# First two pieces' q, k, v loaded into the last weights' space, weights prepared wide and in place, and a new order of the opening

## The chip, the core and the metric

The kernel runs on one core of a Trainium2 chip (trn2). The metric is the device time of one execution in microseconds. Matmuls run on TensorE (PE, with its weight loads as PEld), element-wise work on VectorE (DVE), ScalarE (ACT) and GpSimd (POOL); all loads and stores are issued from SyncE's queue (SP).

## What is computed

Three stages follow each other: windowed attention, a gated MLP behind an RMS norm, and a second MLP with a softmax-like gate and a layer norm. The weights come as 64-bit floats, since a 32-bit array is scaled by a NumPy 64-bit scalar.

```python
# attention: B, H, S, D = 4, 8, 576, 64
scores = scale * np.matmul(q, k.transpose(0, 1, 3, 2))
mask_plain = (rel >= 0) & (rel < 32)                       # heads 0 to 3
mask_dil = (rel >= 0) & (rel < 128) & (rel % 4 == 0)       # heads 4 to 7
attn = softmax(np.where(masks, scores, -1e9)); out = attn @ v
# first MLP: 2304 tokens, 512 -> 1536 -> 512
xn = x / np.sqrt(np.mean(x * x) + 1e-6) * rms_g
y = (silu(xn @ w_gate) * (xn @ w_val)) @ w_out
# second MLP: 512 -> 1024 -> 512
h = y @ w_in;  solu = h * softmax(h)
out = ((solu - mean) / sqrt(var + 1e-6) * g_ln) @ w_out
```

## The kernel before

The 2304 tokens are cut into nine **pieces** of 256 (line 26). The attention of a piece is done in groups of eight heads' query blocks; a group is one load of q and k, one load of v, and a chain: `scores` (TensorE, into PSUM `sp`), `maximum`, `centred`, `exps`, `sums`, `norm`, `weights`, `transposes` (TensorE, `tp`), two scaled copies `turned0` and `turned1` (`pT`), `values` (TensorE, `pv`), `copy` into `x`. The pieces 0 and 1 have four groups each, with a mask added by a matmul (`first`); they are the opening. `rms` then squares `x`, sums over the model's width with matmuls (`ms`), takes the root on GpSimd, spreads it over the partitions with a matmul (`rs`), scales `x`, and splits it into a high and a low part (`xh`, `xl`) in fp32r, so that a product in full precision is three matmuls (`mm3`, lines 603 to 606).

The first MLP works on 12 blocks f of 128 hidden units. For each f there are `g` and `vp` (the two input products, one PSUM bank each), then tanh on ScalarE, two products and the high-low split on VectorE and ScalarE (`u`, `uh`), and `y` (the output product). The table `VIRTUAL` says which tokens and f go together: piece 0 with f=0 to 2 at 256 columns, piece 1 with f=0 to 2, then both together with f=3 to 11 at 512 columns, then the later pieces. The attention of the later pieces is spread between these matmuls.

The weights are in 64 bits and are turned on the chip, in 36 blocks of 512 (f times gate, value, output), by `prepare`: a fetch of 512 KB (`raw_w`), `shifted` on ScalarE (high words, into `tf`), `parts` on VectorE (low words shifted right, into `wf`; line 276), `joined` on VectorE (line 280), `halves` on ScalarE (the high part, `h_w`), and `lows` on VectorE or GpSimd (the difference; line 250, the helper `less`). `tf` and `wf` have two and four buffers. The second MLP's 16 blocks go the same way, each after the last use of the block whose space it takes.

The order on every engine is set by a **planner**, `Plan`: each step has a list of steps that it needs, buffers that it takes, a cost on each engine that may do it and a due time; the planner runs these through a list schedule and writes the instructions in the order that comes out. Each engine works its instructions strictly in that order. While the planner expects TensorE to be idle, ahead of the first `spread`, the main loop writes filler matmuls (`warm`, line 858) into its stream. q, k and v have two buffers each, so the third group's load waits for the first group's scores.

Of the kernel before, what the change touches and what calls it, by code (L numbers as in the profile page):

```python
# [105 lines left out]
class Plan:  # L106
# [3 lines left out]
    SLACK = {"t": 0.3, "s": 0.2}  # L110
# [12 lines left out]
    def order(self):  # L123
# [73 lines left out]
def tile_attention_glu_solu(ctx: ExitStack, tc: tile.TileContext, qk_d, v_d, w1_d, win2_d, wout2_d,  # L197
# [20 lines left out]
    seed = const.tile([P, 1], BF16, name="seed")  # L218
    rmsg = const.tile([P, KD], F32, name="rmsg")
# [9 lines left out]
                 "sq": 2, "rs": 1, "u": 2, "uh": 2, "yo": 2, "wf": 4, "bh": 1, "bl": 1, "ch": 1, "cl": 1,  # L229
                 "yl": 3, "yh": 3} | {f"w{f}_{i}": 1 for f in range(NF1) for i in range(3)})  # L230
# [25 lines left out]
    def prepare(key, tag, src, scale, due, needs=()):
        k, raw, tf, wf, th = ((x, key) for x in ("k", "raw", "tf", "wf", "th"))

        def fetch(e):
            r = T[raw] = wp.tile([P, 512, 2], I32, tag=tag, name=f"raw_{tag}")  # L260
            nc.sync.dma_start(out=r.rearrange("p n t -> p (n t)"), in_=src.bitcast(I32))

        def shifted(e):


            nc.scalar.activation(new(stg, tf, [P, 512], name="tf"), T[raw][:, :, 1].bitcast(F32), AF.Prelu,
                                 scale=2.0 ** -112, alpha=-2.0 ** 32)

        def wf_():
            return T["wf", key[0]][:, plan.where[wf][1]]  # L270

        def parts(e):

            if ("wf", key[0]) not in T:
                T["wf", key[0]] = xn.tile([P, 4, 512], F32, tag="cl0", name="wf")
            nc.vector.tensor_scalar(wf_().bitcast(U32), T[raw][:, :, 0].bitcast(U32), 29, None, ALU.logical_shift_right)

        def joined(e):
            w = wf_().bitcast(U32)
            nc.vector.scalar_tensor_tensor(out=w, in0=T[tf].bitcast(U32), scalar=3, in1=w,  # L280
                                           op0=ALU.logical_shift_left, op1=ALU.bitwise_or)

        def scaled(e):
            put(e, wf_(), wf_(), scale)

        def halves(e):

            T[th] = wp.tile([P, 2, 512], F32R, tag=tag, name=f"h_{tag}")
            put(e, T[th][:, 0], wf_())

        def lows(e):
            less(e, T[th][:, 1], wf_(), T[th][:, 0])
            (w1 if key[0] == 1 else w2)[key[1:]] = T[th]

        plan.add((key, "fetch"), {"s": 1.6}, fetch, needs, due=due - 12)
        plan.add((key, "shifted"), {"a": 0.68}, shifted, [(key, "fetch")], takes=[("yo", tf)], due=due)
        lead = (key[0],) + ((0, 0) if key[0] == 1 else (0,))
# [663 lines left out]
```

## Time and profile before

| | |
|---|---|
| median of 3 runs | 780.44 us (779.95 to 780.68) |
| the profiled execution | 782.46 us, span 780.7 us |
| TensorE busy | 98% of the span |
| VectorE, ScalarE, GpSimd busy | 53%, 40%, 14% |
| mean granted TensorE clock | 0.987 |
| read from HBM | 58.71 MB |

The profile is one execution, seen by the hardware profiler. Its span is from the first to the last instruction; the profiled execution's own time is a little longer and stands beside the runs' times. The busy share of TensorE says little here, since matmuls are pipelined and fillers count as work; more is to be read from when a certain matmul starts. The granted clock is the share of full clock that TensorE got in a stretch.

### The profile page before, as it was taken

To read this page: it belongs to the slowest core of one execution; us is meant where nothing else is said; L and a number is where in the kernel's file an instruction comes from. 1 tells how busy PE (TensorE), PEld (TensorE's weight loads), DVE (VectorE), ACT (ScalarE), POOL (GpSimd) and SP (SyncE) were. 2 spreads that over 40 slices of the span, in tenths; PEclk is the share of its full clock that TensorE was granted. 3 is DMA by queue.
4 is the path that set the end of the run, shared out by engine and by line. 5 is a ranking of instruction groups with operands and counts; after the bars stand their busy time and mean duration, and the time that the engine had idled before them with its cause. 6 is when DMAs were issued, how large, how long until landed. Compare 5 with 4: busy or idle time off the path is not lost.

```text
span 780.7 us, 12092 instructions
## 1 busy us (share of the span) xinstructions
PE 763.8 (98%) x4775; PEld 634.7 (81%) x4775; DVE 416.3 (53%) x838; ACT 315.8 (40%) x781; POOL 111.2 (14%) x150
## 2 busy tenths in 40 slices
PE   8799999999999999999999999999999999999997
PEld 6689887789997778887788888888878888888886
DVE  4769999754444344434353438962254445444542
ACT  3456676444333333324333325531144433434432
POOL 0121033321120121211110200200011101101100
PEclk9869999999999999999999999999999999999999
DMA  8999022242014201033211027500101101111101
GB/s 260 318 384 372 22 73 72 76 130 73 14 33 134 71 27 49 1 100 124 73 41 50 1 83 241 176 28 0 68 1 54 55 28 54 54 29 55 40 28 41
DMA packets 34234, 68.94 MB, mean 88 GB/s; under 512 B 3329, under 2 KB 13569, under 8 KB 34177
## 3 DMA queue, kind: packets, MB, share of 16 engines
q1 hardware_dynamic: 34176, 68.16, 26.1%
q8 instruction: 38, 0.62, 0.3%
q14 instruction: 20, 0.16, 0.1%
HBM read 58.71 MB, written 9.44 MB: 87 GB/s over the span
## 4 chain that ended last, share of the span: by engine, by line
PE 89%; DVE 5%; DMA 2%; issue 1%; ACT 1%; POOL 1%; SPq 0%; ACTq 0%; POOLq 0%; DVEq 0%
PE vp L604 7%; PE y L604 6%; PE vp L606 6%; PE vp L605 6%; PE g L604 6%; PE y L605 6%; PE g L606 6%; PE y L606 6%; PE g L605 6%; PE h L745 4%; PE h L743 4%; PE h L744 4%; PE o L784 4%; PE o L783 4%; PE o L782 4%; PE pv L416 3%
## 5 line engine op out<-in xcount | busy, mean ns | idle before, releaser
L604 PE MATMUL y<-uh,h_w 128*128 128x512 f32 (+1 forms) x252 | 94.0, 373 | 1.0 <-ACT uh L241 1.0
L605 PE MATMUL y<-uh,h_w 128*128 128x512 f32 (+1 forms) x252 | 91.4, 363 | 0.1
L606 PE MATMUL y<-uh,h_w 128*128 128x512 f32 (+1 forms) x252 | 91.2, 362 | 0.0
L640 DVE SCALAR_TENSOR_TENSOR u<-u,g 128x512 f32<-128x512 f32 (+1 forms) x63 | 38.4, 610 | 94.1 <-ACT u L634 93.7
L604 PE MATMUL vp<-xh,h_w 128*128 128x512 f32 (+1 forms) x204 | 81.7, 400 | 0.0
L604 PE MATMUL g<-xh,h_w 128*128 128x512 f32 (+1 forms) x204 | 79.5, 390 | 0.0
L606 PE MATMUL g<-xh,h_w 128*128 128x512 f32 (+1 forms) x204 | 77.7, 381 | 0.3 <-POOL h_w L250 0.3
L605 PE MATMUL g<-xl,h_w 128*128 128x512 f32 (+1 forms) x204 | 77.7, 381 | 0.2 <-DVE xl L250 0.2
L606 PE MATMUL vp<-xh,h_w 128*128 128x512 f32 (+1 forms) x204 | 77.7, 381 | 0.0
L605 PE MATMUL vp<-xl,h_w 128*128 128x512 f32 (+1 forms) x204 | 77.6, 380 | 0.0
L634 ACT ACTIVATE u<-g 128x512 f32<-128x512 f32 (+1 forms) x63 | 33.9, 538 | 85.6 <-PE g L606 85.2
L241 ACT CAST uh<-u 128x512 fp32r<-128x512 f32 (+1 forms) x63 | 35.3, 560 | 74.0 <-DVE u L644 73.9
L644 DVE SCALAR_TENSOR_TENSOR u<-u,vp 128x512 f32<-128x512 f32 (+1 forms) x63 | 38.4, 609 | 47.6 <-PE vp L606 47.4
L381 ACT ACTIVATE s<-s,nm 128x64 f32<-128x64 f32 x120 | 40.6, 341 | 47.9 <-DVE nm L367 47.9
L743 PE MATMUL h<-h_w,yh 128*128 128x512 f32 x144 | 58.2, 404 | 0.0
L784 PE MATMUL o<-h_w,lt 128*128 128x512 f32 (+1 forms) x152 | 57.9, 381 | 0.2 <-DVE lt L772 0.2
L782 PE MATMUL o<-h_w,lt 128*128 128x512 f32 (+1 forms) x152 | 57.7, 380 | 0.0
L783 PE MATMUL o<-h_w,lt 128*128 128x512 f32 (+1 forms) x152 | 57.6, 379 | 0.0
L745 PE MATMUL h<-h_w,yh 128*128 128x512 f32 x144 | 57.0, 396 | 0.0
L744 PE MATMUL h<-h_w,yh 128*128 128x512 f32 x144 | 56.8, 395 | 0.0
L604 PEld LDWEIGHTS y<-uh,h_w 128*128 128x128 f32 x252 | 48.0, 191 | 9.1 <-ACT uh L241 1.2
L500 POOL TENSOR_TENSOR sq<-x 128x256 f32<-128x256 f32 x30 | 19.4, 650 | 249.9 <-DVE x L245 211.0
(115 smaller groups left out, 1552.6 us busy)
## 6 DMA issues: line engine op xcount, KB each, us to landing
raw_w<-w SPq DMA_DIRECT2D x36, 512.0 KB, 10.1
vt<-v SPq DMA_DIRECT2D x38, 256.0 KB, 3.0
qk<-qk SPq DMA_DIRECT2D x20, 400.0 KB, 4.0
y<-yT SPq DMA_DIRECT2D x18, 256.0 KB, 3.0
yT<-yo SPq DMA_DIRECT2D x16, 256.0 KB, 2.3
raw_w<-win SPq DMA_DIRECT2D x8, 512.0 KB, 4.7
raw_w<-wout SPq DMA_DIRECT2D x8, 512.0 KB, 4.3
out<-ob SPq DMA_DIRECT2D x16, 256.0 KB, 2.1
```

Of the source, the lines that this page charges most:

```text
L381: nc.scalar.activation(T[s_][:, i], (T[sp] if first else T[s_])[:, i], AF.Exp, scale=0.125 if first else 1.0, bias=st["nm"][:, i:i + 1], a ...
L604: nc.tensor.matmul(acc, wh, xh, start=first, stop=False)
L605: nc.tensor.matmul(acc, wh, xl, start=False, stop=False)
L606: nc.tensor.matmul(acc, wl, xh, start=False, stop=last)
L640: return lambda e: nc.vector.scalar_tensor_tensor(out=u_of(f), in0=u_of(f), scalar=1.0, in1=T["g", v, f], op0=ALU.add, op1=ALU.mult)
L644: return lambda e: nc.vector.scalar_tensor_tensor(out=u_of(f), in0=u_of(f), scalar=0.5, in1=T["vp", v, f], op0=ALU.mult, op1=ALU.mult)
L743: nc.tensor.matmul(h[:, n], yh[:, 0, k], w[:, 0], start=(k == 0), stop=False)
L744: nc.tensor.matmul(h[:, n], yh[:, 0, k], w[:, 1], start=False, stop=False)
L745: nc.tensor.matmul(h[:, n], yh[:, 1, k], w[:, 0], start=False, stop=(k == KD - 1))
L782: nc.tensor.matmul(o, lt[:, 0, k], w[:, 0], start=(k == 0), stop=False)
L783: nc.tensor.matmul(o, lt[:, 0, k], w[:, 1], start=False, stop=False)
L784: nc.tensor.matmul(o, lt[:, 1, k], w[:, 0], start=False, stop=(k == NF2 - 1))
```

## The change

1. **Loads.** The q, k and v of the first eight groups no longer use the two buffers of the pool but lie in the space of the weights w8 to w11 (`EARLY`), four blocks of the plan's `early_tile`. The loads of w8 to w11 wait for the scores and values that read there; the load of w7 waits for the first piece's split, since that piece's `x` lies in w7's space.
2. **Weights in place.** `shifted` and `parts` write their result over the raw words; `tf` is gone. From f=7 on (`SINGLE`) the three blocks of an f are one tile and each step works on 1536 elements at once. `wf` has two buffers of four blocks. The second MLP's fetches wait for `out` of the f whose space they take.
3. **First piece in PSUM.** Its four `values` results stay in two PSUM banks (`stays`); squares and scalings read them there, and there is no `copy`. All its groups use the `split` form (centre, then one exponential, then a sum). `high` and `low` of `x` work on two of the four blocks at once, for all pieces.
4. **Fillers.** `fill` puts fillers into the bank of the operation that follows, up to 75 us of the plan's time, and adds zeros where the bank is accumulating.
5. **Order.** New costs, due times and slack in the planner; a step's lag to a follower now counts only between engines.

```diff
+EARLY = {(t, n): (NF1 - 1 - 2 * t - n // 2, n % 2) for t in range(2) for n in range(4)}
+X_AT = 7
+SINGLE = 7
+SLACK = {"t": 0.25, "a": 0.4, "d": 0.05, "p": 0.25, "s": 0.2}
+DUE_GROUP, DUE_NEXT, DUE_NORM, DUE_WEIGHTS, DUE_SLOT, DUE_THIRD = (0, 10), 2.23, (7.8, 22.2), 1.47, 4.73, 31.97
+FILL = 75.0
...
+    def fill(x, add=False):
+
+        while filling[0] > 0:
+            filling[0] -= 1
+            nc.tensor.matmul(x, (nothing if add else seed)[:, 0:1].to_broadcast([P, P]),
+                             seed.to_broadcast([P, x.shape[1]]), start=not add, stop=not add)
...
+        def word(c, x):
+            return raw(c)[:, :, :, x]
+
+        def shifted(c):
+
+
+            return lambda e: nc.scalar.activation(word(c, 1).bitcast(F32), word(c, 1).bitcast(F32), AF.Prelu,
+                                                  scale=2.0 ** -112, alpha=-2.0 ** 32)
+
+        def parts(c):
+
+            return lambda e: nc.vector.tensor_scalar(word(c, 0).bitcast(U32), word(c, 0).bitcast(U32), 29, None,
+                                                     ALU.logical_shift_right)
+
+        def joined(c):
+            return lambda e: nc.vector.scalar_tensor_tensor(
+                out=wf_(c).bitcast(U32), in0=word(c, 1).bitcast(U32), scalar=3, in1=word(c, 0).bitcast(U32),
+                op0=ALU.logical_shift_left, op1=ALU.bitwise_or)
...
+            plan.add((key, "lows", n), {"p": pool_, "d": two}, lows(c), [(key, "halves", n)], uses=[wf, st, (st, 1)], due=due)
...
-        split = first and n % 2 == 0
+        split = first and (t == 0 or n % 2 == 0)
+        stays = t == 0
...
         def load_qk(e):
-            tile_ = new(at, qk, [P, QK_MAX])
+            if first:
+                T[qk] = early_tile()[:, 1024 * EARLY[K][1]:1024 * EARLY[K][1] + 1024]
+            tile_ = T[qk] if first else new(at, qk, [P, QK_MAX])
...
-            x = new_bank(pv, [P, TP], "pv")
+            if stays:
+                if n % 2 == 0:
+                    new_bank(("pvs", n), [P, 2, TP], "pv")
+                x = T[pv] = T["pvs", n - n % 2][:, n % 2]
+            else:
+                x = new_bank(pv, [P, TP], "pv")
+            fill(x)
...
+                    nc.vector.scalar_tensor_tensor(
+                        out=in_order(T[x][:, k], k), in0=by_set(T["pv", (t, source[k])], k), scalar=rmsg[:, k:k + 1],
+                        in1=in_order(st["rs"], k), op0=ALU.mult, op1=ALU.mult)
...
         def high(k):
-            return lambda e: put(e, place(0, k), T[x][:, k])
+            return lambda e: put(e, place(0, k), T[x][:, 2 * k:2 * k + 2])
...
-            prepare((1, f, i), f"w{f}_{i}", w1_d[f, :, i * 512:(i + 1) * 512], None, 14 + 2.72 * (3 * f + i))
+        prepare(1, f, [(0,), (1,), (2,)] if f < SINGLE else [(0, 1, 2)],
+                [w1_d[f, :, i * 512:(i + 1) * 512] for i in range(3)], [None] * 3,
+                [DUE_WEIGHTS + DUE_SLOT * (3 * f + i) for i in range(3)],
+                [(x, K) for K, (at_f, _) in EARLY.items() for x in ("scores", "values") if at_f == f] +
+                [("low", k, 0) for k in range(2) if f == X_AT])
...
-                for _ in range(int((at_ - free) / 0.13) if warm is not None else 0):
-                    nc.tensor.matmul(warm[:, 0:256], seed.to_broadcast([P, P]), seed.to_broadcast([P, 256]),
-                                     start=True, stop=True)
+                filling[0] = int((at_ - free) / 0.13) if at_ < FILL else 0
                 free = at_ + plan.steps[name]["engines"]["t"]
                 if name[0] == "spread":
                     warm = None
+                if warm is not None:
+                    fill(warm)
```

SyncE's queue at the start, before (`qk` and `vt` are a group's loads, `raw_w` a weight block):

```order
L808 DMA masks<-mask 128x704
L337 DMA qk<-qk 128x800
L341 DMA vt<-v 128x512
L808 DMA ident<-ident 128x128
L337 DMA qk<-qk 128x800
L341 DMA vt<-v 128x512
L337 DMA qk<-qk 128x800
L261 DMA raw_w_0_163<-w 128x1024
L337 DMA qk<-qk 128x800
L808 DMA gln<-gln 128x8
```

The same queue after (`qkv` is the space in w8 to w11):

```order
L294 DMA raw_0_107<-w 128x1024
L917 DMA masks<-mask 128x704
L402 DMA qkv<-qk 128x800
L409 DMA qkv<-v 128x512
L294 DMA raw_1_116<-w 128x1024
L402 DMA qkv<-qk 128x800
L917 DMA ident<-ident 128x128
L409 DMA qkv<-v 128x512
L402 DMA qkv<-qk 128x800
L409 DMA qkv<-v 128x512
```

The first weight block has moved from eighth place to the first and the second to the fifth.

VectorE ahead of the second piece's last `xl`, before (`r` and `rd` are the norm, `u` and `uh` the element-wise steps of an f, L276 and L280 a weight block's shift and join):

```order
L530 TENSOR_SCALAR rd<-ident,r 128x128 x2
L276 TENSOR_SCALAR wf<-raw_w_2_467 128x512
L280 SCALAR_TENSOR_TENSOR wf<-tf,wf 128x512
L640 SCALAR_TENSOR_TENSOR u<-u,g 128x256
L542 SCALAR_TENSOR_TENSOR x<-x,rmsg,rs 128x256 x2
L644 SCALAR_TENSOR_TENSOR u<-u,vp 128x256
L542 SCALAR_TENSOR_TENSOR x<-x,rmsg,rs 128x256
L250 TENSOR_TENSOR uh<-u,uh 128x256
L250 TENSOR_TENSOR xl<-x,xh 128x256 x2
L542 SCALAR_TENSOR_TENSOR x<-x,rmsg,rs 128x256
L245 CAST xh<-x 128x256
L250 TENSOR_TENSOR xl<-x,xh 128x256
```

The same place after:

```order
L314 TENSOR_SCALAR raw_2_510<-raw_2_510 128x512
L265 TENSOR_TENSOR w_1_758<-wf,w_1_758 128x512
L625 TENSOR_SCALAR rd<-ident,r 128x128 x2
L318 SCALAR_TENSOR_TENSOR wf<-raw_2_510 128x512
L749 SCALAR_TENSOR_TENSOR u<-u,g 128x256
L647 SCALAR_TENSOR_TENSOR x<-x,rmsg,rs 128x256 x2
L753 SCALAR_TENSOR_TENSOR u<-u,vp 128x256
L647 SCALAR_TENSOR_TENSOR x<-x,rmsg,rs 128x256
L265 TENSOR_TENSOR xl<-x,xh 128x2x256
L265 TENSOR_TENSOR uh<-u,uh 128x256
L647 SCALAR_TENSOR_TENSOR x<-x,rmsg,rs 128x256
L260 CAST xh<-x 128x2x256
```

The last block joined ahead of the second piece's `xl` was w1_2 (the sixth) and is now w2_2 (the ninth), and the element-wise steps of f=2 of the first piece now stand ahead of it too.

## Rows read from the trace of the kernel before

**Rows 1.** The page's part 2: granted TensorE clock, 40 slices.

```profile
PEclk9869999999999999999999999999999999999999
```

**Rows 2.** Busy time by stretch, for each engine (instructions), clock, DMA share, GB/s.

```profile
0.00:10.00 10.00, 9.12 (x79) 6.84 (x80) 2.00 (x8) 1.91 (x3) 0.59 (x9) 1.00 0.64 191
10.00:20.00 10.00, 8.74 (x127) 6.51 (x126) 7.25 (x23) 5.18 (x22) 0.61 (x1) 1.00 0.96 334
20.00:30.00 10.00, 7.58 (x97) 6.34 (x94) 5.91 (x19) 3.95 (x15) 1.40 (x2) 0.83 0.95 297
30.00:40.00 10.00, 7.52 (x81) 6.17 (x79) 8.15 (x23) 5.64 (x19) 1.56 (x3) 0.84 0.86 315
40.00:50.00 10.00, 9.41 (x68) 9.07 (x66) 6.37 (x16) 5.25 (x13) 0.00 (x1) 0.50 1.01 390
50.00:60.00 10.00, 8.92 (x57) 8.47 (x56) 7.67 (x20) 4.37 (x10) 2.99 (x3) 0.81 1.03 410
60.00:70.00 10.00, 9.73 (x79) 9.37 (x79) 9.60 (x19) 6.56 (x14) 1.43 (x1) 1.00 1.03 410
```

**Rows 3.** TensorE in order of time: start, duration, operation [idle before].

```profile
25.00 0.69 PE L352 MATMUL sp<-qk 128*64 128x64 f32 x16 [2.42 <-DMA qk<-qk]
...
33.50 0.39 PE L604 MATMUL g<-xh,h_w 128*128 128x256 f32 x1
...
37.16 1.12 PE L416 MATMUL pv<-pT,vt 128*64 128x64 f32 x16 [2.24 <-DVE x L245]
...
52.21 0.41 PE L605 MATMUL g<-xl,h_w 128*128 128x256 f32 x1
...
52.42 0.41 PE L606 MATMUL g<-xh,h_w 128*128 128x256 f32 x1
...
59.11 0.28 PE L604 MATMUL g<-xh,h_w 128*128 128x256 f32 x1
59.23 0.28 PE L605 MATMUL g<-xl,h_w 128*128 128x256 f32 x1
...
75.72 0.40 PE L604 MATMUL g<-xh,h_w 128*128 128x512 f32 x1
```

**Rows 4.** The same view, the first fillers.

```profile
0.88 5.95 PE L858 MATMUL warm<-seed 128*128 128x256 bf16 x30 [0.88 <-POOL half L848]
...
7.49 1.51 PE L858 MATMUL warm<-seed 128*128 128x256 bf16 x12
```

**Rows 5.** The same view, VectorE: the first maximum, a weight block's shift and join.

```profile
7.60 0.42 DVE L362 TENSOR_REDUCE nm<-sp 128x4 f32<-128x256 f32 x1 [6.58 <-PE sp L352]
...
42.20 0.42 DVE L276 TENSOR_SCALAR wf<-raw_w 128x512 uint32<-128x512 uint32 x1
42.65 0.69 DVE L280 SCALAR_TENSOR_TENSOR wf<-tf,wf 128x512 uint32<-128x512 uint32 x1
```

**Rows 6.** Groups by line, VectorE, 0 to 77 us: busy us, mean ns.

```profile
L250 DVE TENSOR_TENSOR h_w<-wf,h_w 128x512 fp32r<-128x512 f32 x10 | 6.9, 688 | 0.3 <-ACT h_w L241 0.2
L542 DVE SCALAR_TENSOR_TENSOR x<-x,rmsg,rs 128x256 f32<-128x256 f32 x8 | 3.5, 474 | 1.2 <-PE rs L533 1.2
L640 DVE SCALAR_TENSOR_TENSOR u<-u,g 128x256 f32<-128x256 f32 x6 | 2.5, 416 | 1.1 <-ACT u L634 1.1
...
L389 DVE TENSOR_SCALAR rn<-sm 128x4 f32<-128x4 f32 x8 | 1.3, 165 | 0.1
L530 DVE TENSOR_SCALAR rd<-ident,r 128x128 f32<-128x128 f32 x4 | 1.0, 283 | 0.6 <-POOL r L525 0.6
...
L245 DVE CAST xh<-x 128x256 fp32r<-128x256 f32 x2 | 0.6, 294 | 0.1
```

**Rows 7.** GpSimd's differences, 0 to 160 us by line; one and VectorE in time.

```profile
L250 POOL TENSOR_TENSOR h_w<-wf,h_w 128x512 fp32r<-128x512 f32 x10 | 13.9, 1389 | 49.5 <-ACT h_w L241 49.5
...
61.35 1.43 POOL L250 TENSOR_TENSOR h_w<-wf,h_w 128x512 fp32r<-128x512 f32 x1 [3.98 <-ACT h_w L241]
...
61.93 1.14 DVE L276 TENSOR_SCALAR wf<-raw_w 128x512 uint32<-128x512 uint32 x1
```

More of the change, by code (lines that the diff above doesn't have):

```diff
@@ L176, in order @@
                 left[key].discard(name)
-                last[key] = max(last.get(key, 0.0), start + cost + lag)
+                last[key] = max(last.get(key, 0.0), start + cost + self.LAG[e])
                 if not left[key] and key in where:
@@ L250, in less @@
         ENG[e].tensor_tensor(dst, a, b, ALU.subtract)
-    w1, w2 = {}, {}
[L256 to L297, printed above, removed]
-        plan.add((key, "parts"), {"d": 0.42}, parts, [(key, "fetch")] + [(lead, "parts")] * (key != lead),
-                 takes=[("wf", wf)] + [("cl", ("stage", key[0]))] * (key == lead), uses=[("stage", key[0])], due=due)
-        plan.add((key, "joined"), {"d": 0.72}, joined, [(key, "parts"), (key, "shifted")], uses=[tf], due=due)
-        before = "joined"
-        if scale is not None:
-            plan.add((key, "scaled"), {"d": 0.45, "p": 0.92}, scaled, [(key, "joined")], due=due)
-            before = "scaled"
-        plan.add((key, "halves"), {"a": 0.62}, halves, [(key, before)], due=due)
-        plan.add((key, "lows"), {"p": 1.6, "d": 1.0}, lows, [(key, "halves")], uses=[wf, ("stage", key[0])], due=due)
@@ L481, in rms, with in_order, by_set @@
         gs = GROUPS[t]
+        stays = t == 0
+        source = {g["dst"]: n for n, g in enumerate(gs)}
+        def in_order(y, k):
+            if gs[source[k]]["kind"] == "plain":
+                return y
+            return y.rearrange("p (r q c) -> p c r q", r=2, c=4)
+        def by_set(y, k):
+            return y if gs[source[k]]["kind"] == "plain" else y.rearrange("p (c r q) -> p c r q", c=4, r=2)
         whole = {k: max(n for n, g in enumerate(gs) if g["kind"] in ("both", "tail") and k > 1 or
@@ L532, in spread @@
         def spread(e):
-            nc.tensor.matmul(bank(a_spread, [P, TP], "rs"), ones, T["rd", t], start=True, stop=True)
+            x = bank(a_spread, [P, TP], "rs")
+            fill(x)
+            nc.tensor.matmul(x, ones, T["rd", t], start=True, stop=True)
         def keep(e):
@@ L566, in rms @@
         for k in ks:
-            plan.add(step("square", k), {"a": 0.42, "d": 0.42, "p": 0.75} if first else {"p": 0.7}, square(k),
-                     [("copy", (t, n)) for n in range(whole[k] + 1)], takes=[("sq", ("sq", t, k))], uses=[x], due=due)
+            plan.add(step("square", k), {"a": 0.42} if stays else {"a": 0.42, "d": 0.42, "p": 0.75} if first else {"p": 0.7},
+                     square(k), [("values", (t, source[k]))] if stays else [("copy", (t, n)) for n in range(whole[k] + 1)],
+                     takes=[("sq", ("sq", t, k))], uses=[("pvs", source[k] - source[k] % 2)] if stays else [x], due=due)
             if first:
@@ L666, in outs @@
             return emit
[L668 removed]
+        ready = [(x, k, t) for t in pieces for k in range(2) for x in ("high", "low")]
         ys = [("y", p, k) for k in range(KD)]
```

174 lines of the change are left out of this document (126 added, 48 removed).

## Prediction

> **What bounds the kernel now.** I read the clock line of the slices first, then the table of stretches, then TensorE's own order of time, and last the costs on VectorE. From about 54 us on, TensorE is the bound and hardly ever waits: the clock line is at 9 to the end [rows 1], and the stretch 60 to 70 us has 9.73 us of it busy [rows 2]. What the change touches lies in front of that. A good mark for the end of the opening is the first matmul of 512 columns, `g` of f=3 for pieces 0 and 1 together, which starts at 75.72 us [rows 3]. By then TensorE has run 204 matmuls of 256 columns (f=0 to 2 for two pieces are 216, less the last twelve `y`) and eight attention groups. The 204 cost 0.12 us each at full clock (from 59.11 to 59.23), 24.5 us [rows 3]. The other 51 us are the small matmuls of attention, fillers, waiting and slow clock. What comes behind the mark, 780.7 - 75.7 = 705.0 us, is the same matmuls in nearly the same order after the change, so **the result is the shift of this mark**.
>
> Three things make the opening long. Transfers: TensorE stands 2.42 us for the seventh group's q and k, whose buffer came free late [rows 3]; the stretches from 10 to 40 us move 297 to 334 GB/s where 390 to 410 is reached later [rows 2]. VectorE: it holds 7.25, 5.91, 8.15, 6.37 and 7.67 us of work in the five stretches from 10 to 60 us, 35.35 of 50, or 71%, since its inputs come late, and is nearly full (9.60) from 60 us [rows 2]. The clock: behind the 2.24 us wait of `pv` on the copy of `x` [rows 3] the granted share falls to 0.50 for the whole stretch 40 to 50 us [rows 2], and a 256-column matmul then takes 0.21 us (52.21 to 52.42) and not 0.12 [rows 3]. Those are TensorE's two levels, 1.2 and 2.4 GHz.
>
> **The change part by part.** *Loads.* The q, k and v of the first eight groups go into space of w8 to w11, so none waits for a buffer. Counted in SP's new order, the eighth group's q and k are the 22nd transfer (two tiny tables aside), with 8.1 MB up to and with them. The first 10 us move 1.9 MB [rows 2]; the other 6.2 MB take 15 us at 410 GB/s and 19 us at 334, so they land at 25 to 29 us, and the seventh group's 1.2 MB sooner, at 22 to 25 us, against the 25.00 us at which its scores start now [rows 3]. The price is at the front: the first weights (512 KB) now go ahead of mask and q, k. 39 fillers stand ahead of the first scores, where 30 took 5.95 us and the next twelve 1.51 us, 0.13 each [rows 4]: nine more are 1.1 us. The first maximum, at 7.60 us now [rows 5], comes at about 8.5 us, and the 1.1 MB ahead of it have landed by then. The w7 and w8 to w11 loads wait for the end of the first pieces, but have eight transfers queued ahead of them; f=7 is needed some 35 us behind the mark, so I cost that at nothing, and at most at 1 us.
>
> *VectorE up to the first piece's normalised x.* Behind the first maximum its order has five whole groups (maximum, centring, sums and weights at 0.42, the two [128,4] steps at 0.17 each: 2.0) = 10.1; the sixth 1.4 and the seventh 1.6; four shifts and two joins of weights, 4x0.42 + 2x0.69 = 3.1; the norm 0.17 + 2x0.28 + 0.42, four scalings at 0.47, two casts at an estimated 0.43 (0.29 for half the width) and two differences at 0.69 = 5.3 [rows 5, 6]. The sum is **21.5 us**. The first piece's copies out of PSUM are gone, and the transposed probabilities of both pieces now go to ScalarE; what that makes VectorE wait is counted below.
>
> *VectorE up to the second piece's x.* Six joins 4.1, four shifts 1.7, three weight differences 2.1, nine element-wise steps at 0.42 for f=0 to 2 of the first piece 3.8, the eighth group 1.4, two copies and a square 1.3, the norm 0.7, four scalings 1.9, cast and differences 1.8 [rows 5, 6]: **18.8 us**. Without any wait the second x is complete at 8.5 + 21.5 + 18.8 = 48.8 us. It now has three weight blocks more ahead of it than before, which is why its fill matters.
>
> *GpSimd.* Five weight differences move to it in front of that point (w0_1, w0_2, w1_1, w2_0, w2_2). One takes 1.39 us [rows 7], off the path in itself. But the trace shows what it does to VectorE: while GpSimd holds 61.35 to 62.78, a shift of 0.42 takes 1.14 us [rows 7]. I take that row's 0.72 for each of the five, 3.6 us; the bounds are 0 and the whole 1.39, 7.0 us. The Trainium skill, SBUF — State Buffer, section "Who interferes with whom", says that these two engines take a shared port pair exclusively, for a whole instruction; the row agrees in kind, and the rule alone would put the sum at the 7.0 end.
>
> *In-place shift.* It now writes every second word; the row that reads every second word and writes dense takes 0.42 for 512 [rows 5]. No row writes so. The nearest rows bound it: 0.42, and the join of the same width, 0.69 [rows 5]; I take 0.42, since the read side is the same pattern. The other end costs 9x0.27 = 2.4 us. The Trainium skill, VectorE: DVE Perf Modes, "What auto-detection actually checks", makes the double rate depend on one source and both ends in SBUF, with no word on a step, which sides with 0.42; no run here shows it. The wide forms (three blocks at once from f=7) come behind the mark, where VectorE is then ahead; I cost them at nothing, at most some tenths either way.
>
> *Waits of VectorE.* In the walk group by group it still waits for the exponentials, for two transposes and for q, k of groups six and seven. I take 3 us over the 40; the bounds are 0 and what the present fill of 71% makes of it, 16 us. So the second x: 48.8 + 3.6 + 3 = **55.4 us**.
>
> *From there to the mark.* The order has 96 matmuls of 256 columns in between (36 `g`, 36 `vp`, 24 `y`): 96x0.12 = 11.5, and 1.1 for three fillers and for `g`, which has one bank, to be read by tanh and the first product. The mark comes at **68.0 us**, 7.7 earlier. The first x is there at about 8.5 + 21.5 + 3 = 33 us, as against the first `g` at 33.50 now [rows 3]. From there f=0 to 2 of the first piece (108x0.12 = 13 us) and the rest of attention (two `pv` of at most 1.12 [rows 3], and smaller ones, 2 to 3 us) run in the 22 us in which VectorE goes on to the second x, so they cost nothing as long as the clock holds; 14 of the 118 fillers stand there or later, where all 97 stood ahead of the first `g` before.
>
> Second-stage weights are asked for one or two matmul groups later, six f ahead of their use, and the rest of the order differs by which half of a product a transpose stands in: 0, at most 1 us either way.
>
> **The rivals.** (a) *No waits, little blocking*: second x at 49 to 53, mark at 61.5 to 65.5, 766 to 770. For it: the transfers are really out of the way. Against it: no stretch ahead of 60 us is over 82% full now [rows 2]. (b) *GpSimd blocks for its whole length*: 3.4 us more, mark 71.4, **776.1**. This is the rule named above, as it would act here; the one row shows half. (c) *The clock falls again* when TensorE waits for the second x. For it: the drop behind 2.24 us of waiting, and few fillers there. A spell from the first `g` on and as long as the one now, which covers the 40 to 50 row and parts of both beside it (some 17 us), costs half its length, 8.5 us, against some 5 that TensorE has to spare: 3.5 to 4 us, **776.5**. (d) *Nothing gained*: The change does not do what it is arranged for: VectorE, with more to do ahead of the second x, is only 74% full, which puts that x at 8.5 + 40.3/0.74 = 63.0 and the mark at 75.6: **780.3**. (e) *Slower*: the three more weight blocks are ahead of the second x, and VectorE goes on waiting as in 10 to 60 us. At 71% the 40.3 us take 56.8, x comes at 65.3, the mark at 77.9, **782.6**. It turns from gain to loss at a fill of 74%. Against it: a good part of those 29% was the late q, k and TensorE at half clock, which the change goes at. A half-clock spell of over 26 us (26/2 less 5 to spare = 8) would do the same.
>
> **How the numbers follow.** The profiled execution took 782.46 with a span of 780.7; the median of the runs is 780.44, and I set the shift against that: 780.44 - 7.7 = 772.7. Chances: forecast (mark 65.5 to 70.5, 770.2 to 775.2) 0.54; (a) 0.10; (b) 0.08; (c) 0.08; (d) 0.07; (e) 0.13. About 0.2%, 1.6 us, is what a measurement of this kernel can tell from no change. Faster: 0.54 + 0.10 + 0.08 + 0.08 = 0.80; same 0.07; slower 0.13. The range for 8 in 10 takes the forecast, (b), (c) and the near part of (a), and a little of the way to (d): 767.0 to 779.0.
>
> **What would show it.** The first 512-column `g` at 65.5 to 70.5 us and the rest of the span near 705 us; no wait of TensorE on q, k over 1 us; VectorE at 80 to 90% from 10 to 55 us; its steps stretched by about 0.7 us where GpSimd makes a weight difference; the in-place shift at 0.42; a granted clock near 1 from 10 us on. It is wrong if the clock stays at 0.50 for several stretches between 34 and 60 us, if the second x comes later than 60 us, or if the time behind the mark changes by over 2 us.

## The result, and the profile after

The changed kernel takes **769.13 us** (768.97 to 769.26, 4 runs), the kernel before in the same session 780.56 us (779.95 to 781.57, 4 runs): 11.4 us less, ratio 0.9852, 95% interval 0.9835 to 0.9869. The profiled execution took 768.97 with a span of 767.2.

The granted clock in 40 slices, part 2 of the page of the changed kernel, against [rows 1]:

```profile
PEclk9999999999999999999999999999999999999999
```

Its stretches, for [rows 2]: us; busy time (instructions) of PE, PEld, DVE, ACT, POOL; granted clock, DMA share, GB/s.

```profile
0.00:10.00 10.00, 8.70 (x75) 6.80 (x77) 3.95 (x11) 3.88 (x6) 0.62 (x10) 1.00 0.80 278
10.00:20.00 10.00, 8.46 (x141) 6.80 (x143) 9.04 (x25) 6.10 (x14) 1.28 (x1) 1.00 1.04 394
20.00:30.00 10.00, 7.98 (x124) 6.13 (x121) 8.59 (x26) 6.96 (x22) 2.58 (x3) 1.00 1.03 402
30.00:40.00 10.00, 8.74 (x95) 8.01 (x95) 7.68 (x18) 7.30 (x22) 1.78 (x2) 1.00 1.03 407
40.00:50.00 10.00, 9.77 (x90) 9.31 (x89) 9.60 (x22) 7.78 (x16) 3.24 (x4) 1.00 1.02 407
50.00:60.00 10.00, 10.00 (x87) 9.74 (x86) 9.36 (x20) 9.15 (x17) 1.67 (x2) 1.00 1.03 410
...
80.00:100.00 20.00, 20.00 (x143) 16.01 (x143) 19.42 (x27) 10.66 (x27) 6.68 (x2) 1.00 0.20 62
100.00:120.00 20.00, 20.00 (x144) 15.95 (x143) 19.15 (x28) 10.83 (x31) 5.80 (x4) 1.00 0.25 72
120.00:140.00 20.00, 20.00 (x145) 15.85 (x144) 11.59 (x26) 8.57 (x32) 6.96 (x8) 1.00 0.24 77
```

VectorE works 44.27 of the 50 us from 10 to 60, 89% where it was 71%. The transfers run at 394 to 407 GB/s where they ran at 297 to 334, and the clock stays at 2.4 GHz. TensorE is full from 70 us on. The last three rows matter below: VectorE is 96 to 97% busy until 120 us and only then has time.

TensorE in order of time (start, duration, operation, [idle before]), for [rows 3, 4]:

```profile
0.88 5.90 PE L274 MATMUL warm<-seed 128*128 128x256 bf16 x39 [0.88 <-POOL half L961]
...
22.60 0.69 PE L421 MATMUL sp<-qkv 128*64 128x64 f32 x16
25.80 0.69 PE L421 MATMUL sp<-qkv 128*64 128x64 f32 x16
...
65.02 0.40 PE L712 MATMUL g<-xh,w 128*128 128x512 f32 x1
...
67.34 0.39 PE L713 MATMUL y<-uh,w 128*128 128x256 f32 x1 [0.67 <-DVE uh L265]
```

The seventh and eighth groups' scores start at 22.60 and 25.80 us; the seventh's were at 25.00 before [rows 3], and it no longer waits 2.42 us. The first 512-column `g` is at 65.02, not 75.72: **10.7 us earlier**, of which 0.7 goes at once into the wait at 67.34.

To see where time goes behind that mark, compare the same instruction in both traces. The tanh behind `g` of f = 3, 6, 9 and 11 of the first two pieces, and the last tanh of the first stage, on ScalarE, before:

```profile
80.31 0.60 ACT L634 ACTIVATE u<-g 128x512 f32<-128x512 f32 x1
104.49 0.60 ACT L634 ACTIVATE u<-g 128x512 f32<-128x512 f32 x1 [0.54 <-PE g L606]
135.57 0.60 ACT L634 ACTIVATE u<-g 128x512 f32<-128x512 f32 x1 [0.47 <-PE g L606]
157.19 0.60 ACT L634 ACTIVATE u<-g 128x512 f32<-128x512 f32 x1 [2.82 <-PE g L606]
551.38 0.60 ACT L634 ACTIVATE u<-g 128x512 f32<-128x512 f32 x1 [4.16 <-PE g L606]
```

and after:

```profile
70.41 0.60 ACT L743 ACTIVATE u<-g 128x512 f32<-128x512 f32 x1
94.59 0.60 ACT L743 ACTIVATE u<-g 128x512 f32<-128x512 f32 x1 [2.36 <-PE g L714]
124.70 0.60 ACT L743 ACTIVATE u<-g 128x512 f32<-128x512 f32 x1 [0.61 <-PE g L714]
145.04 0.60 ACT L743 ACTIVATE u<-g 128x512 f32<-128x512 f32 x1 [0.62 <-PE g L714]
540.30 0.60 ACT L743 ACTIVATE u<-g 128x512 f32<-128x512 f32 x1 [4.16 <-PE g L714]
```

The gain is 9.9 us at 80 and at 104, 10.9 at 136, 12.2 at 157, and 11.1 at 551 us. So 9.9 us come from the opening, 2.2 more between 104 and 157, and about 1 us is given back later. At the end of the span it is 13.5, but the last 2.4 us belong to that one execution of before, which took 782.46 against a median of 780.44. From the last tanh to the end it needed 229.3 us, where the changed kernel needed 226.9, and so did the kernel before with other fillers, below, which has before's instructions there. What counts is the 11.1, and the medians say 11.4.

### The profile page after: what moved, and what is told of

Same layout as the page of the kernel before. It is cut to its first block, busy times and chain, and to the rows that moved or that the text cites. A ratio compares the mean times of both kernels' runs of the same rounds, so it can differ in the third digit from the quotient of the medians.

```text
span 767.2 us, 11984 instructions
## 1 busy us (share of the span) xinstructions
PE 754.5 (98%) x4796; PEld 627.3 (82%) x4796; DVE 406.5 (53%) x803; ACT 310.2 (40%) x735; POOL 105.3 (14%) x131
## 4 chain that ended last, share of the span: by engine, by line
PE 92%; DVE 3%; DMA 3%; ACT 1%; issue 0%; SPq 0%; POOL 0%; ACTq 0%; DVEq 0%; POOLq 0%
PE vp L712 7%; PE y L712 7%; PE g L712 6%; PE y L713 6%; PE vp L714 6%; PE vp L713 6%; PE y L714 6%; PE g L714 6%; PE g L713 6%; PE o L893 4%; PE h L854 4%; PE h L852 4%; PE h L853 4%; PE o L891 4%; PE o L892 4%; DMA qkv<-qk 3%
## 5 line engine op out<-in xcount | busy, mean ns | idle before, releaser
L712 PE MATMUL y<-uh,w 128*128 128x512 f32 (+1 forms) x252 | 93.1, 369 | 0.0
L713 PE MATMUL y<-uh,w 128*128 128x512 f32 (+1 forms) x252 | 90.7, 360 | 0.8 <-DVE uh L265 0.8
L714 PE MATMUL y<-uh,w 128*128 128x512 f32 (+1 forms) x252 | 90.6, 360 | 0.0
L712 PE MATMUL vp<-xh,w 128*128 128x512 f32 (+1 forms) x204 | 81.0, 397 | 0.0
L712 PE MATMUL g<-xh,w 128*128 128x512 f32 (+1 forms) x204 | 79.9, 392 | 0.0
L714 PE MATMUL vp<-xh,w 128*128 128x512 f32 (+1 forms) x204 | 77.3, 379 | 0.0
L714 PE MATMUL g<-xh,w 128*128 128x512 f32 (+1 forms) x204 | 77.2, 378 | 0.0
L713 PE MATMUL vp<-xl,w 128*128 128x512 f32 (+1 forms) x204 | 77.1, 378 | 0.0
L713 PE MATMUL g<-xl,w 128*128 128x512 f32 (+1 forms) x204 | 76.9, 377 | 0.0
L893 PE MATMUL o<-w,lt 128*128 128x512 f32 (+1 forms) x152 | 57.8, 380 | 0.2 <-DVE lt L881 0.2
L891 PE MATMUL o<-w,lt 128*128 128x512 f32 (+1 forms) x152 | 57.7, 380 | 0.0
L892 PE MATMUL o<-w,lt 128*128 128x512 f32 (+1 forms) x152 | 57.5, 378 | 0.0
L852 PE MATMUL h<-w,yh 128*128 128x512 f32 x144 | 57.4, 399 | 0.0
L853 PE MATMUL h<-w,yh 128*128 128x512 f32 x144 | 56.1, 390 | 0.0
L854 PE MATMUL h<-w,yh 128*128 128x512 f32 x144 | 56.1, 390 | 0.0
L713 PEld LDWEIGHTS y<-uh,w 128*128 128x128 f32 x252 | 47.6, 189 | 8.0 <-DVE uh L265 1.3
L256 ACT ACTIVATE pT<-tp,half 128x256 f32<-128x256 f32 x76 | 32.1, 470 | 54.4 <-PE tp L469 54.0
```

Of the source, the lines that this page charges most:

```text
L256: nc.scalar.copy(dst, src) if scale is None else nc.scalar.mul(dst, src, scale)
L712: nc.tensor.matmul(acc, wh, xh, start=first, stop=False)
L713: nc.tensor.matmul(acc, wh, xl, start=False, stop=False)
L714: nc.tensor.matmul(acc, wl, xh, start=False, stop=last)
L852: nc.tensor.matmul(h[:, n], yh[:, 0, k], w[:, 0], start=(k == 0), stop=False)
L853: nc.tensor.matmul(h[:, n], yh[:, 0, k], w[:, 1], start=False, stop=False)
```

## The experiments

Shifts are those of the tanh of f = 5 and f = 11 of the first two pieces, against the changed kernel (84.85 and 145.04 us). They are used where a microsecond counts, since the kernel before spread from 776.95 to 786.78 us in these sessions. The ratio is to before in the same session, with its 95% interval. The order on the engines is the changed kernel's only in the runs whose expectation says so; in "two buffers", "copies", the three with old numbers and "wide from f=5" the planner made a new order, so that more differs there than the part named.

| kernel | median us | ratio to before | first 512-column g | shift f=5 | shift f=11 |
|---|---|---|---|---|---|
| before | 780.56 | 1 | 75.72 | +9.9 | +12.2 |
| changed | 769.13 | 0.9852 (0.9835 to 0.9869) | 65.02 | 0 | 0 |
| front fillers only | 769.89 | 0.9855 (0.9827 to 0.9884) | 66.30 | +1.6 | +1.5 |
| before, filled | 776.75 | 0.9946 (0.9924 to 0.9968) | 73.43 | +7.4 | +9.6 |
| two buffers | 777.72 | 0.9954 (0.9935 to 0.9973) | 69.72 | +4.4 | +9.5 |
| no wide form | 772.03 | 0.9885 (0.9858 to 0.9912) | 64.72 | -0.3 | +2.3 |
| joins twice, front | 770.58 | 0.9858 (0.9829 to 0.9887) | 67.62 | +2.6 | +2.6 |
| GpSimd lows twice | 772.49 | 0.9885 (0.9856 to 0.9913) | 67.94 | +3.0 | +2.9 |
| copies | 773.49 | 0.9895 (0.9868 to 0.9923) | 67.55 | +1.6 | +5.2 |
| old numbers | 779.44 | 0.9966 (0.9940 to 0.9993) | 73.85 | +8.7 | +12.9 |
| old weight dues | 780.13 | 1.0005 (0.9979 to 1.0031) | 68.70 | +2.8 | +10.8 |
| old slack, lags | 775.82 | 0.9925 (0.9897 to 0.9952) | 71.08 | +5.8 | +8.4 |
| joins twice, behind | 774.32 | 0.9906 (0.9874 to 0.9937) | 65.28 | +0.3 | +4.7 |
| wide from f=5 | 775.70 | 0.9924 (0.9896 to 0.9951) | 64.98 | -0.3 | +6.5 |

### The clock: two runs

Front fillers only: the changed kernel keeps the fillers ahead of its first scores and loses the others.

```diff
-FILL = 75.0
+FILL = 7.0
```

> The changed kernel with the same order on every engine, but fillers only ahead of the first scores (39); the other 79 are left out. Theory A, VectorE sets the opening and the clock only matters where it makes VectorE wait: TensorE has time to spare there, the mark (first 512-column g) stays at 65 to 67 us, 769 to 771 us. Theory B, the gain is mostly full clock from 40 us on: without fillers the granted clock falls to 0.50 ahead of 40 us and stays there for 10 us or more, the mark comes at 70 us or later, 774 us or more.

Its stretches, same view:

```profile
10.00:20.00 10.00, 9.32 (x112) 7.77 (x111) 8.45 (x23) 4.97 (x12) 1.27 (x1) 0.52 1.04 393
20.00:30.00 10.00, 9.40 (x113) 7.19 (x115) 6.86 (x23) 6.64 (x21) 2.59 (x3) 0.67 1.03 402
30.00:40.00 10.00, 7.54 (x70) 6.45 (x67) 8.70 (x20) 7.89 (x23) 0.17 (x1) 0.61 1.02 407
40.00:50.00 10.00, 9.77 (x91) 9.34 (x90) 9.59 (x20) 6.99 (x15) 3.94 (x4) 1.00 1.03 408
```

The clock falls as much as Theory B wants, to 0.52, 0.67 and 0.61 for 30 us, and still the tanh of f = 11 comes only 1.5 us later. That is Theory A: TensorE had the rest of that time to spare. The profiled execution is the slowest of the four; by the medians, 769.89 and 769.13, the cost is 0.8 us.

Before, filled: the other way round, the changed kernel's filler rule alone.

```diff
-                for _ in range(int((at_ - free) / 0.13) if warm is not None else 0):
-                    nc.tensor.matmul(warm[:, 0:256], ...)
+                filling[0] = int((at_ - free) / 0.13) if at_ < 75.0 else 0
...
+            fill(x)    # ahead of scores, transposes, values, spread, g and vp, y
```

> The kernel before with its own order, loads and engines, but with the changed kernel's rule for fillers (into whatever bank comes next, up to 75 us of the plan). Theory A: the stretch 40 to 50 us is at 1.00 and not 0.50, but VectorE's work and its late inputs set the mark, which moves by 1 to 3 us only: 777.5 to 779.5 us. Theory B, the clock carries the gain: the mark comes 5 us or more earlier, 775 us or less.

The mark moved by 2.3 us (75.72 to 73.43), as Theory A has it; the stretch from 40 to 50 us rose from 0.50 to 0.67 only, not to 1.00. The median is 0.75 us under the range, 3.8 under before's 780.56. With the other run: full clock is worth 0.8 to 1.5 us where it is taken from the changed kernel, and 2.5 (in the traces) to 3.8 us (by the medians) where it is given to the kernel before. That is a part of the 11, not the most of it. In six of the runs that follow (two buffers, joins twice in front, copies, and the three with old numbers) the clock fell in the opening too, for 10 to 30 us and not below 0.66 in any stretch of 10 us, so a part of their shifts is the clock's; by the first run of this section I estimate that part at 1.5 us or less.

### The early loads

The eight groups' q, k and v go back into two buffers:

```diff
-            if first:
-                T[qk] = early_tile()[:, 1024 * EARLY[K][1]:1024 * EARLY[K][1] + 1024]
-            tile_ = T[qk] if first else new(at, qk, [P, QK_MAX])
+            tile_ = new(at, qk, [P, QK_MAX])
...     # v likewise
```

> The changed kernel with q, k and v of the first eight groups back in the pool's two buffers (the order is planned anew for that). Theory A, early loads are what lets VectorE fill up: TensorE waits over 1 us for q, k again, VectorE is at 80% or less from 10 to 60 us, the mark comes 3 to 6 us later, 772 to 775 us. Rival: the order alone hides the loads, 768.5 to 770.5 us, VectorE still at 87% or more.

The mark comes 4.7 us later, inside Theory A's 3 to 6; TensorE again waits for q, k, the longest time 1.65 us. VectorE's fill did not fall to 80% (it is 43.98 of 50, 88%). The total is 2.7 us over the range, because another 5 us are lost *behind* the mark, which neither theory had. TensorE, same view as above:

```profile
110.94 0.41 PE L464 MATMUL tp<-ident,s 128*128 128x128 f32 x2 [1.59 <-DVE s L457]
122.16 0.66 PE L464 MATMUL tp<-ident,s 128*128 128x128 f32 x2 [2.66 <-DVE s L457]
```

These are transposes of the third piece's probabilities, which VectorE delivers late. A part of that is GpSimd's doing: in this order it makes two of the wide weight differences, from 97.93 and from 111.64 us, where the changed kernel has one. Beside them a wide shift on VectorE lasts 3.66 us, not 0.95, and a wide join 4.57, not 1.75 (the section on GpSimd and the one on why the prediction was right come back to this). The wait at `tp` returns in seven of the nine runs that follow.

### VectorE behind the mark: two runs

No wide form: each step on three blocks sent as three, in the same order (shown for the join).

```diff
-            return lambda e: nc.vector.scalar_tensor_tensor(
-                out=wf_(c)..., in0=word(c, 1)..., scalar=3, in1=word(c, 0)..., ...)
+            return lambda e: [nc.vector.scalar_tensor_tensor(
+                out=wf_(c)[:, j]..., in0=word(c, 1)[:, j]..., scalar=3, in1=word(c, 0)[:, j]..., ...)
+                for j in range(len(c))]
```

> The changed kernel with each wide preparation step of three weight blocks sent as three steps, in the same order. Theory A, what TensorE gained behind the mark (705.0 to 702.2 us) comes from the earlier loads and the new order, not from the wide form: the mark stays at 65 us, VectorE has 4 to 6 us more to do up to 130 us and TensorE still doesn't wait for it, 769 to 770 us. Rival, the wide form frees VectorE in time: TensorE waits again between 115 and 160 us, the rest of the span is back at 704 to 706 us, 771 to 773 us.

Theory A is wrong. The mark stays (64.72), but VectorE, with 3.0 us more to do in the whole span (409.5 against 406.5), makes TensorE wait:

```profile
97.14 0.41 PE L471 MATMUL tp<-ident,s 128*128 128x128 f32 x2 [1.57 <-DVE s L464]
...
106.09 0.41 PE L471 MATMUL tp<-ident,s 128*128 128x128 f32 x2 [0.38 <-DVE s L464]
...
117.64 0.41 PE L471 MATMUL tp<-ident,s 128*128 128x128 f32 x2 [0.27 <-DVE s L464]
```

The sum is 1.57 + 0.38 + 0.27 = 2.2 us, the whole shift of 2.3. The time is the rival's, though the waits begin some 20 us earlier than the rival put them.

Joins twice, behind the mark:

```diff
+                              for _ in range(2 if stage == 1 and f in (7, 8) else 1)]
```

> The changed kernel, same order, with the wide join of f=7 and f=8 done twice on VectorE (1.75 us each, 3.5 us in all, behind the mark). Theory A, VectorE is still the bound behind the mark until about 120 us: the mark stays at 65.0 us, TensorE waits there for the third piece's probabilities, 2 to 3.5 us later in all, 771 to 772.5 us. Rival, VectorE is ahead of TensorE there and has slack (the prediction's step): 769 to 769.7 us.

Theory A is right in kind, but the price is higher: 3.5 us of work cost 4.7 us (0.3 of them ahead of the mark). GpSimd adds to it. GpSimd and VectorE, in order of time, in this kernel:

```profile
88.76 5.03 POOL L265 TENSOR_TENSOR w<-wf,w 128x1536 fp32r<-128x1536 f32 x1 [22.55 <-ACT w L256]
...
90.47 4.94 DVE L318 SCALAR_TENSOR_TENSOR wf<-raw 128x1536 uint32<-128x1536 uint32 x1
95.33 0.67 DVE L754 SCALAR_TENSOR_TENSOR u<-u,vp 128x512 f32<-128x512 f32 x1
```

The repeated join takes 4.94 instead of 1.75 us: it ends at 95.41, 1.6 after GpSimd's wide difference (88.76 + 5.03 = 93.79), as if it had only then begun. In the changed kernel the same GpSimd instruction holds up another step by less (3.23 instead of 1.75 us, shown further down). Over the whole span VectorE is busy 4.6 us longer (411.1 against 406.5), about the shift.

### VectorE ahead of the mark

The joins of the first six weight blocks are done twice:

```diff
+                              for _ in range(2 if stage == 1 and f < 2 else 1)]
```

> The changed kernel, same order, with the join of the first six weight blocks done twice on VectorE (0.69 us each, 4.1 us in all ahead of the second x; two of them ahead of the first x). Theory A, VectorE's work sets the opening: the first 512-column g comes 3.5 to 4.5 us later (68.5 to 69.5 us against 65.0) and the whole 772.5 to 773.5 us. Rival, transfers or the chain of groups set it and VectorE has slack: under 1.5 us later, under 770.5 us.

The result lies between the two: 2.6 us for 4.1 us of work. Three of the joins, not two, lie ahead of the first x, the first of them in time that VectorE has free ahead of its first maximum. The first tanh moved by 1.95 us (37.07 to 39.02), about what these joins take (1.4 us for two, 2.1 for three); the three behind it added only 0.7. An estimated 0.3 of both is a later start of this execution: its first maximum was at 8.93, and "joins twice, behind", which is the changed kernel up to the mark and had its first maximum at 8.84, has its mark 0.3 later. So VectorE is neither the only bound nor free: somewhat over half of what it is given there is on the path, and most of that ahead of the first x.

### GpSimd beside VectorE

Five weight differences on GpSimd are done twice:

```diff
                 less(e, th[:, :, 1], wf_(c), th[:, :, 0])
+                if e == "p" and again[0] > 0:
+                    again[0] -= 1
+                    less(e, th[:, :, 1], wf_(c), th[:, :, 0])
```

> The changed kernel, same order, with each of the first five weight differences on GpSimd done twice (five more instructions of 1.3 us on an engine with time to spare). By the prediction's step (0.72 us of VectorE lost for each): mark 3 to 3.6 us later, 772 to 772.7 us. By blocking for the whole length: 6.5 us later, 775 us or more. Without any blocking: at most 0.7 us later, under 770 us.

The shift is 2.9 us for five instructions of 1.3: 0.58 each, a little under the prediction's 0.72. Blocking for the whole length (6.5) and no blocking are both ruled out for the sum. VectorE's instructions are the same, yet it is busy 3.8 us longer over the span (410.3 against 406.5), so the time goes into steps that are held up; for a weight that comes later TensorE waits only 0.37 us.

### Heads kept in PSUM

The first piece's heads are copied out of PSUM again:

```diff
-        stays = t == 0
+        stays = False
```

> The changed kernel with the first piece's heads copied out of PSUM into x as before (planned anew; squares may go to three engines again). Theory A: four copies of about 0.45 us come back, in part on VectorE, and the keep and the wider scalings go; mark 0.5 to 2 us later, 769.5 to 771 us. Rival, keeping the heads in PSUM takes the wait of TensorE on the copies away and is a main part of the gain: 772 us or more.

The time is the rival's, but not for its reason. The mark is 2.5 us later, a little over Theory A's 2, the tanh of f = 5 only 1.6 later, and up to there TensorE waits for no copy. The rest of the 5.2 comes behind it, again at `tp` (waits of 1.27 us at 97.37 and 1.80 at 118.82). VectorE has 1.0 us more to do over the span (407.5 against 406.5), but the new order also gives GpSimd a second wide difference, at 110.15 us, ahead of the second wait. Which of the two it is isn't shown.

### The planner's numbers: three runs

Old numbers: slack, lags and due times together. All three of these kernels also let a filler ahead of `y` add zeros in one more case (`f > 0 or c0 > 0`).

```diff
-SLACK = {"t": 0.25, "a": 0.4, "d": 0.05, "p": 0.25, "s": 0.2}
+SLACK = {"t": 0.3, "a": 0.25, "d": 0.25, "p": 0.25, "s": 0.2}
-DUE_GROUP, ..., DUE_THIRD = (0, 10), 2.23, (7.8, 22.2), 1.47, 4.73, 31.97
+DUE_GROUP, ..., DUE_THIRD = (0, 10), 2.5, (9, 19), 14, 2.72, 60
-... done[n][1] + (self.LAG[e_] if (e_ := done[n][0]) != e or e == "s" else 0.0)
+... done[n][1] + self.LAG[done[n][0]]
```

> The changed kernel with the planner's slack, lags and due times of the kernel before (loads, places, engines to choose from and wide forms as changed). Theory A, the early loads and VectorE's lighter work carry the gain, the order only a part: VectorE at 80% or more from 10 to 60 us, 2 to 5 us later than the changed kernel, 771 to 774 us. Rival, the order carries it: VectorE under 76%, 776 us or more.

The time is the rival's, though VectorE's fill is Theory A's (40.74 of 50, 81%). With every other part of the change in place, the old numbers leave at most 3 us of the 11: by the ratio of its session 2.7, by the tanh of f = 11, which comes later than before's, none. Theory A, that the order is only a part, is wrong.

Old weight dues: of these, only 1.47 and 4.73 back to 14 and 2.72.

> The changed kernel with only the due times of the weight blocks put back (first block due at 14 us of the plan and each next 2.72 us later, where the change has 1.47 and 4.73). Theory A: the early due times give VectorE weight steps to do in the gaps of the first groups; without them it does less than 8 us of work in 10 to 20 us, has weight blocks left over for the stretch ahead of the second x, and the mark comes 4 us or more later: 773.5 us or more. Rival: slack and lags carry the order's part, 771 us or less.

Theory A is right about 10 to 20 us (VectorE does 7.64 us of work, in the changed kernel 9.04) and about the total; the mark is 3.7 us later, just short of its 4. But 8.1 of the 10.8 us are lost behind the tanh of f = 5, 4.70 of them in one wait:

```profile
111.68 0.66 PE L469 MATMUL tp<-ident,s 128*128 128x128 f32 x2 [4.70 <-DVE s L462]
```

The step that it waits for is held up by GpSimd. GpSimd and VectorE in this kernel:

```profile
107.84 3.42 POOL L265 TENSOR_TENSOR w<-wf,w 128x1536 fp32r<-128x1536 f32 x1 [0.99 <-ACT w L256]
...
107.99 3.54 DVE L462 TENSOR_TENSOR s<-s,rn 128x256 f32<-128x256 f32 x1
```

A step of 0.42 us lasts 3.54, to 0.3 us behind GpSimd's end: 3.1 of the 4.70 us. Behind the wait the granted clock is 0.69 from 110 to 120 us, which costs an estimated 3 us more (0.31 of 10). So work that is left over is only a part of this loss; where GpSimd's wide differences fall is another.

Old slack and lags: the other part alone.

> The changed kernel with only the planner's slack and lags put back, due times as changed. Theory A (due times of the weights carry the order's part): VectorE's opening keeps its weight steps between the groups, at most 4 us later than the changed kernel, 769 to 773 us. Rival (slack and lags carry it): 775 us or more.

The rival is right. VectorE has only 4.72 us of work from 30 to 40 us (7.68 in the changed kernel): the first x is complete at 35.9, not 32.1, and then VectorE stands still for a `pv`:

```profile
35.23 0.69 DVE L265 TENSOR_TENSOR xl<-x,xh 128x512 fp32r<-128x512 f32 x1 [1.03 <-ACT xh L256]
...
39.69 0.42 DVE L260 COPY x<-pv 128x256 f32<-128x256 f32 x1 [3.23 <-PE pv L492]
```

The mark is 6.1 us later, and `tp` waits 2.63 us at 112.66. So both parts of the numbers are needed; each undone alone loses most of the gain, and they don't add up (8.4 and 10.8 alone, 12.9 together).

### A version that goes further

The wide form begins two f earlier:

```diff
-SINGLE = 7
+SINGLE = 5
```

> The changed kernel with the wide preparation from f=5 on instead of f=7 (planned anew). VectorE has some 2 us less to do between 40 and 100 us. Theory A: TensorE waits only 0.7 us for VectorE there in the changed kernel, so at most that is gained, 768 to 769.5 us. Rival: three blocks at once keep VectorE from the third piece's steps and from f=5 on time, 771 us or more.

The rival is right: 6.6 us worse. VectorE has fewer instructions from 40 to 100 us (88, in the changed kernel 100) but is busy longer (58.26 us, 57.49), since GpSimd takes two more wide differences and each of the three holds up a wide shift. GpSimd and VectorE in this kernel:

```profile
87.31 3.48 POOL L265 TENSOR_TENSOR w<-wf,w 128x1536 fp32r<-128x1536 f32 x1 [12.58 <-ACT w L256]
...
87.74 3.87 DVE L314 TENSOR_SCALAR raw<-raw 128x1536 uint32<-128x1536 uint32 x1
```

and TensorE:

```profile
97.73 0.41 PE L469 MATMUL tp<-ident,s 128*128 128x128 f32 x2 [2.25 <-DVE s L462]
...
110.64 0.66 PE L469 MATMUL tp<-ident,s 128*128 128x128 f32 x2 [3.00 <-DVE s L462]
```

A wide shift of 0.95 us lasts 3.87; beside the other two it lasts 2.85 and 3.66. No version here beats the changed kernel.

## Why the prediction was right, point by point

The time lies inside the range of 767.0 to 779.0, on the side named, 3.6 us under the forecast. It is not in the forecast's own band, though: mark and time, 65.02 and 769.13, lie just below 65.5 to 70.5 and 770.2 to 775.2, where rival (a) had them, with a chance of 0.10. Rival (a)'s reason, no waits and little blocking, is not what happened: both were there, the waits larger than forecast. The sum came out near because two errors ran against each other, so its closeness is in part luck. Its steps:

**The result is the shift of the mark.** This is true for most of it: the mark moved by 10.7 us, 9.9 of that reach f = 3 to 6, and the whole is 11.4. "705.0 behind the mark" did not hold in its parts. In the two profiles it went from 705.0 to 702.2, by more than the 2 us that the prediction named as a sign of being wrong; 2.4 of these 2.8 us are the slower end of that one execution of before. Ahead of it 2.2 us are gained and 1.1 given back. The gain is in part this, TensorE before:

```profile
133.26 0.41 PE L399 MATMUL tp<-ident,s 128*128 128x128 f32 x2 [0.97 <-DVE s L393]
...
148.22 0.69 PE L416 MATMUL pv<-pT,vt 128*64 128x64 f32 x16 [0.50 <-DVE x L245]
```

VectorE held TensorE up twice. In the changed kernel TensorE stands for no more than 0.2 us at a time between 68 and 160 us.

**Transfers.** Right: eighth group at 25.80 (25 to 29 forecast), seventh at 22.60 (22 to 25), no wait of over 1 us (the longest is 0.76), and 4.4 us of the opening hang on it, as far as a run with a new order can tell.

**The first maximum at 8.5 us** (+1.1 for nine fillers). It came at 7.55, since the 39 fillers took only 5.90 us. But the term is not on the path: in the run with joins behind the mark the same opening had its first maximum at 8.84 and the mark at 65.28, 0.26 later.

**VectorE's work up to the second x.** The sum was right and its use was not. Sum with blocking: 21.5 + 18.8 + 3.6 = 43.9; the 98 rows from 7.55 us to the end of that x at 52.83 add up to 43.6. But VectorE is busy for only 39.6 us there, since an instruction that doesn't need the one before starts ahead of its end. VectorE in order of time, changed kernel:

```profile
41.51 0.69 DVE L318 SCALAR_TENSOR_TENSOR wf<-raw 128x512 uint32<-128x512 uint32 x1
42.12 0.42 DVE L749 SCALAR_TENSOR_TENSOR u<-u,g 128x256 f32<-128x256 f32 x1
42.45 0.42 DVE L314 TENSOR_SCALAR raw<-raw 128x512 uint32<-128x512 uint32 x1
42.79 0.42 DVE L260 COPY x<-pv 128x256 f32<-128x256 f32 x1
```

Starts are 0.61, 0.33 and 0.34 apart where the rows last 0.69, 0.42 and 0.42. Against that **the waits** were 45.3 - 39.6 = 5.7 us and not 3, the longest 1.85 for ScalarE's cast of a weight block. The two errors leave 45.3 us where 46.9 stood, 1.6 less, and with the 0.95 of the first maximum the second x comes at 52.8, not 55.4.

**From there to the mark.** 12.6 forecast, 12.2 measured. The last low of the first x is done at 32.1 (33 forecast).

**GpSimd.** 3.6 us were taken. Doubling measured 0.58 each, 2.9, and the changed kernel's own rows agree: beside the five differences steps of VectorE last 0.87, 0.81, 0.39, 0.86 and 0.03 us longer than elsewhere, 3.0 in all. The reading behind it was wrong, though. The row of half the length [rows 7] looks like half blocking; but the shift ends at 61.93 + 1.14 = 63.07, 0.29 after GpSimd (62.78). It was held to the end and merely came when half was over, as the join at 90.47 above came well after GpSimd's start. Nor is every step held: in the rows below those with a PSUM operand, and a reduction, are not. GpSimd's wide difference of the changed kernel, and VectorE beside it:

```profile
87.63 4.59 POOL L265 TENSOR_TENSOR w<-wf,w 128x1536 fp32r<-128x1536 f32 x1 [21.70 <-ACT w L256]
```

```profile
88.75 0.68 DVE L753 SCALAR_TENSOR_TENSOR u<-u,vp 128x512 f32<-128x512 f32 x1
89.35 0.64 DVE L260 COPY x<-pv 128x256 f32<-128x256 f32 x1
89.82 0.42 DVE L425 SCALAR_TENSOR_TENSOR s<-sp,masks 128x256 f32<-128x256 f32 x1
90.27 0.42 DVE L436 TENSOR_REDUCE nm<-s 128x4 f32<-128x256 f32 x1
90.61 3.23 DVE L265 TENSOR_TENSOR w<-wf,w 128x1536 fp32r<-128x1536 f32 x1
```

The product, the copy and the masking read PSUM and run at 0.68, 0.64 and 0.42; the difference, both inputs in SBUF, lasts to 93.84, 1.62 after GpSimd's end at 92.22. The Trainium skill, SBUF — State Buffer, section "SBUF: two separate sides", says just this: the pair is claimed by a VectorE step with two SBUF inputs or in a two-port mode, and the later one waits out the whole instruction. The trace agrees. The prediction's rival (b) took the rule to hit every VectorE step, which is more than the page states, and so took 7.0 us where 2.9 to 3.0 were measured.

**In-place shift at 0.42.** Right: 0.42 at 42.45, above.

**The clock.** It stayed up; where it was made to fall, it cost 0.8 to 1.5 us, less than rival (c)'s 3.5 to 4.

**Behind the mark "VectorE is then ahead", wide forms "at nothing".** This step failed. VectorE is 93% full or more until 120 us, and TensorE asks it there for the third piece's probabilities. Without the wide forms 2.3 us are lost, with 3.5 us more work 4.4. The number came out well because this stretch was served in time, not because it had room. In this the prediction was lucky.

**What the sum did not hold: the order.** It was counted through what stands ahead of the second x. The runs show it decides more than that: early due times give VectorE weight steps in the gaps of the first groups, and what is not worked off there comes due at 97 to 122 us, together with the steps that GpSimd's wide differences hold up. Why slack and lags weigh as much was followed only as far as the first x and the wait for `pv` behind it. The 1.1 us that the changed kernel gives back goes with slack and lags too: from the tanh of f = 11 to the last one it is 394.2 us before, 395.3 in the changed kernel, 395.2 with old weight dues alone, and 394.1 and 393.9 in the two runs with old slack and lags. Its mechanism is open.

## What to carry to other kernels

When several edits feed one full engine, the gain is a property of the set: taken out alone, the early loads or the planner's numbers cost 8 to 13 us, and what remains without one of them gains 4 us at most. Look for the next place at which the bound engine waits for the full one, since work that is late in the opening is paid for there (here 30 to 55 us behind the mark), and compare the same instruction in two traces to see where. A fill below 100% ahead of a mark and a full engine behind it mean that work moved behind the mark is paid for nearly in full or dearer (2.3 us for 3.0, 4.4 for 3.5). Work given to GpSimd is not free for VectorE either: a wide difference there, which VectorE is spared, held up one step by 1.5 to 3.2 us.

## What was not expected of the hardware

- VectorE's rows overlap: 98 rows of 43.6 us in 39.6 us of busy time; in the rows shown independent neighbours start 0.08 to 0.09 us ahead of the other's end.
- A GpSimd difference holds up a VectorE step of two SBUF inputs or a shift until its own end, here up to 5 us long: 1.75 became 4.94 us, 0.95 became 3.87, 0.42 became 3.54; steps with a PSUM operand beside it kept 0.64 and 0.68.
- 30 us at a granted share of 0.52 to 0.67 cost 1.5 us of the whole in the trace, 0.8 by the medians.
